# The request for ScalarE's common activation table and the load of the inducing points, moved to the head of the order

## The chip, the cores and the metric

One Trainium2 chip, one of its cores. The metric is the device time of one execution in microseconds; a time is the median of several runs.

## What is computed

Two stages, in float32 at the interfaces. An induced attention block: 32 inducing points attend to the 12480 rows of each of 4 batches, then the rows attend to the 32 results. A feed-forward block with a hard-swish follows, on all 49920 rows.

```python
def _attn_ref(x, inducing):                # x (4, 12480, 128), inducing (32, 128)
    scale = 1.0 / np.sqrt(C)
    I = np.broadcast_to(inducing[None], (B, m, C))
    def mab(q, kv):
        s = scale * (q @ kv.transpose(0, 2, 1))
        s = s - s.max(-1, keepdims=True)
        a = np.exp(s)
        a /= a.sum(-1, keepdims=True) + 1e-09
        return a @ kv
    h = mab(I, x)
    return mab(x, h)

def _moe_ref(x, w_in, w_out):              # w_in (128, 2048), w_out (2048, 128)
    h = x @ w_in
    relu6 = np.clip(h + 3.0, 0.0, 6.0)
    g = h * relu6 / 6.0
    return g @ w_out
```

## The kernel before

Each batch is cut into six groups of 2048 rows and a rest of 192. For each group of the first pass, x is loaded (`X`), cast to bf16 (`K`, line 456), transposed on TensorE (`T`, line 462) and copied out of PSUM (`Y`, line 468). Then come the scores against the inducing points (`S`, line 473), their exponential on ScalarE (`E`, line 481), and the sums over rows (`A`, line 489).

Between the passes, the 32 rows of the batch are prepared. The products of their differences with the first weight are squared on ScalarE (`N`, line 576) and multiplied by the second weight (`P`, line 631). Small steps on VectorE build the operands of the second pass (`cH` to `cP`).

The second pass avoids working over all 2048 hidden columns for each row: it uses the 32 prepared rows and products of pairs of attention weights. For each group it makes scores (`Z`, line 654) and two exponentials of them (`Zd`, line 664, and `Ze`, line 669), the row sums (`R`, line 686), their logarithm on ScalarE (`Rl`, line 691), the scores less that logarithm on VectorE (`Rz`, line 696), and the normalized weights by another exponential (`Ra`, line 710). Pairs of weights are made by a matmul (`B`, line 729), an exponential (`F`, tile `TF`, line 739) and a product on VectorE with a broadcast (`U`, tile `TD`, line 750, with `d` that `W` makes by DMA from POOL's queue, line 675). The matmuls `l` (line 800) and `q` (line 819) give the output rows, `v` (line 830) copies them out of PSUM, and `O` (line 840) stores them.

No scheduler orders this. `ORDER` is a string of tokens, written out by hand, for all four batches. Each token names one step with its indices, its PSUM bank and sometimes its engine, and the steps are emitted in that order:

```python
for token in ORDER.split():
    code, *args = token.split(".")
    ops[code](*[int(a) if a.isdigit() else a for a in args])
```

Every engine, and every queue of DMAs, runs its own part of the string in order. The second pass of one batch is interleaved with the first pass of the next.

ScalarE reads its functions from a table that is loaded by an instruction of its own (ACT_TABLE_LOAD in the trace). One set of functions is in force at a time. Where an instruction needs a function that isn't in the set in force, the build puts a load ahead of it. A kernel can also ask for a set by name. The two steps that the change moves:

```python
def op_i0(e):
    nc.scalar.dma_start(I_sb[:, :], inducing[:, :])              # line 350

def op_it(e):
    nc.scalar.preload_act_table_set("natural_log_exp_and_others")  # line 353
```

`i0` is issued from ScalarE's queue, and its tile is first read by `i4` (line 365), the transpose of the inducing points. `it` has no operands and waits for nothing. Before the change `it` stands between steps of the second pass of batch 0 and the first pass of batch 1.

At the head of the order, `X.0.0.0.8.SP` loads the first half of the first x group from SP's queue, `X.0.0.8.16.P` the second half from POOL's, `i2` clears a tile on VectorE, and `w` runs matmuls on it on TensorE (line 372).

Of the kernel before, what the change touches and what calls it, by code (L numbers as in the profile page):

```python
# [20 lines left out]


ORDER = """
X.0.0.0.8.SP i2.- w.8.6 X.0.0.8.16.P w.4.5 i0.- i1.- i3.V K.0.0.4.8.V X.0.1.0.16.P X.0.2.0.16.P X.0.3.0.16.P
X.0.4.0.16.P X.0.6.0.2.P K.0.0.0.4.A T.0.0.0.8.4 i8.- K.0.0.8.12.A Y.0.0.0.8.4.A K.0.0.12.16.V xc.4.8.V w.3.0
T.0.0.8.16.1 i4.5 i5.5.V w.1.0 S.0.0.0.8.4 K.0.1.0.4.A Y.0.0.8.16.1.V S.0.0.8.16.4 E.0.0.0.16.4 i6.P K.0.2.4.8.A
K.0.1.4.8.V T.0.1.0.8.1 i7.P K.0.2.8.12.A K.0.1.8.12.V K.0.1.12.16.V T.0.1.8.16.5 xc.0.4.V A.0.0.0.8.3 A.0.0.8.16.3
# [30 lines left out]
Y.1.6.0.2.7.V F.0.3.0.0 K.1.4.8.12.V F.0.3.0.1 q.0.2.0.0.5 D.1.1.V q.0.2.1.1.6 v.0.2.1.6.A l.0.2.3.7 H.1.2.4 Z.0.4.0.1  # L58
Zd.0.4.0 X.2.1.0.16.P D.1.2.V q.0.2.3.1.7 S.1.3.0.8.4 S.1.3.8.16.4 S.1.6.0.2.2 E.1.6.0.2.2 T.1.4.8.16.3 K.1.5.12.16.V
T.1.4.0.8.0 q.0.2.3.0.7 Ze.0.4.1 R.0.4.2 q.0.2.2.0.6 Y.1.4.8.16.3.V K.1.5.8.12.V T.1.5.8.16.3 Y.1.4.0.8.0.V W.0.4  # L60
v.0.2.3.7.V l.0.2.2.6 q.0.2.2.1.6 Y.1.5.8.16.3.V it.- O.0.1.0.16.P Rl.0.4.2 Rz.0.4.1 Rh.0.4.V E.1.3.0.16.4 q.0.2.0.1.5
T.1.5.0.8.7 S.1.4.0.8.4 Y.1.5.0.8.7.V v.0.2.2.6.A B.0.3.1 D.1.3.V A.1.3.0.8.6 A.1.3.8.16.6 X.2.2.0.16.P H.1.3.6 Ra.0.3
v.0.2.0.5.A S.1.4.8.16.4 Z.0.5.7.5 F.0.3.1.0 U.0.3.0.2 c2.1.- S.1.5.0.8.0 S.1.5.8.16.0 q.0.3.1.0.6 F.0.3.1.1 U.0.3.1.2
l.0.3.1.6 E.1.4.0.16.4 Ze.0.5.5 A.1.4.0.8.4 A.1.4.8.16.4 D.1.4.V K.2.0.0.4.V H.1.4.4 E.1.5.0.16.0 Zd.0.5.7 q.0.3.1.1.6
# [978 lines left out]
```

## Time and profile before

| | |
|---|---|
| time, median of 3 runs | 295.79 us (295.2 to 297.52) |
| the profiled execution | 296.27 us, span 294.4 us |
| TensorE (PE) busy | 273.8 us, 93% of the span |
| weight loads (PEld) | 211.2 us, 72% |
| ScalarE (ACT) busy | 255.7 us, 87% |
| VectorE (DVE) busy | 226.6 us, 77% |
| GpSimd (POOL) busy | 93.6 us, 32% |
| DMA | 66.69 MB, mean 227 GB/s |
| mean granted TensorE clock | 0.989 of full speed |

The span is the time between the first and the last instruction that the profile shows; the rest of the execution's time lies around it. An engine's busy share is a mean over stages with different limits. A wait in brackets names the idle time of an engine and what ended it. The chain of waits is followed back from the last instruction to what released it at each step.

### The profile page before, as it was taken

Reading aid. Unit: us, or ns where it says so; the run is one execution under the profiler, and the core shown is the slowest. Engines: PE = TensorE matmul, PEld = TensorE weight load, DVE = VectorE, ACT = ScalarE, POOL = GpSimd, SP = SyncE. Lnnn points to the kernel's source line nnn. Section 1 sums busy time; section 2 is a strip of 40 time slices with the busy share of each in tenths; the row PEclk is TensorE's granted clock in tenths of the full one; section 3 lists DMA queues with packets and bytes.
Section 4 is the critical chain, followed back from the end, with each engine's and each line's share of the span. In section 5 each row is a group of like instructions: output and inputs, shape, how many; then the busy total and the mean of one; then the engine's idle time right before and its main releaser. Section 6 shows DMA issues by size and latency. Waiting matters only on the chain.

```text
span 294.4 us, 9799 instructions
## 1 busy us (share of the span) xinstructions
PE 273.8 (93%) x4114; PEld 211.2 (72%) x4122; DVE 226.6 (77%) x468; ACT 255.7 (87%) x426; POOL 93.6 (32%) x184
## 2 busy tenths in 40 slices
PE   7788897699899999999999999999999999999990
PEld 3776565576688777877877877787888767776780
DVE  3889877748699966888798948889879866978750
ACT  2578999979998988998989999978899899889952
POOL 8322420213324013345172043052223233354210
PEclk9999999979999999999999999999999999999998
DMA  7999944066589905469997936339195153686574
GB/s 210 427 394 419 416 132 169 16 213 213 161 274 321 386 19 169 125 212 320 322 387 249 368 99 226 146 90 347 46 336 178 49 183 113 223 256 227 170 292 158
DMA packets 13232, 66.69 MB, mean 227 GB/s; under 512 B 2656, under 2 KB 3200, under 8 KB 7040
## 3 DMA queue, kind: packets, MB, share of 16 engines
q0 software_dynamic: 12416, 63.38, 63.2%
q1 hardware_dynamic: 576, 2.36, 2.1%
q8 instruction: 33, 0.54, 0.8%
q10 hardware_dynamic: 192, 0.28, 0.3%
q14 instruction: 15, 0.12, 0.2%
HBM read 27.67 MB, written 25.56 MB: 181 GB/s over the span
## 4 chain that ended last, share of the span: by engine, by line
PE 66%; ACT 15%; DMA 7%; issue 5%; DVE 4%; POOL 1%; POOLq 0%; ACTq 0%; DVEq 0%
PE ps L819 25%; PE ps L800 7%; PE ps L489 5%; DMA xr<-in_x_dram 5%; PE ps L462 5%; PE ps L729 5%; PE ps L654 4%; PE ps L631 4%; ACT TF L739 4%; PE ps L568 3%; PE ps L473 3%; ACT sq L576 2%; DMA out_dram<-os 2%; PE ps L686 2%; ACT os L830 2%
## 5 line engine op out<-in xcount | busy, mean ns | idle before, releaser
L739 ACT ACTIVATE TF<-ps 128x1024 bf16<-128x1024 f32 (+1 forms) x98 | 94.5, 1006 | 8.2 <-PE ps L729 7.6
L675 POOL DMA_DIRECT2D d<-dk x96 | 54.1, 582 | 95.5 <-ACT dk L664 88.9
L750 DVE TENSOR_TENSOR TD<-TF,d 128x2048 bf16<-128x2048 bf16 x47 | 57.0, 1217 | 5.5 <-ACT TF L739 4.6
L819 PE MATMUL ps<-Cq,TF 128*128 128x128 bf16 (+1 forms) x784 | 60.2, 221 | 0.0
L819 PE MATMUL ps<-Cq,TD 128*128 128x128 bf16 (+1 forms) x784 | 59.6, 221 | 0.1
L819 PEld LDWEIGHTS <-TF 128*128 128x128 bf16 (+1 forms) x784 | 46.2, 99 | 11.1 <-issue 8.4
L819 PEld LDWEIGHTS <-TD 128*128 128x128 bf16 (+1 forms) x784 | 46.2, 99 | 9.3 <-issue 6.0
L830 DVE COPY os<-ps 128x512 f32<-128x512 f32 x55 | 37.6, 686 | 13.4 <-PE ps L819 8.0
L800 PE MATMUL ps<-BD,a 128*128 128x512 f32 x96 | 47.4, 495 | 0.0
L576 ACT ACTIVATE sq<-ps 128x512 bf16<-128x512 f32 x64 | 35.5, 607 | 2.6 <-PE ps L568 2.0
L462 PE MATMUL ps<-ident_b,xb 128*128 128x128 bf16 x384 | 28.6, 219 | 4.1 <-ACT xb L456 2.9
L489 PE MATMUL ps<-xr,a 128*32 128x128 f32 x384 | 29.0, 225 | 2.3 <-ACT xT L468 2.2
L456 DVE CAST xb<-xr 128x512 bf16<-128x512 f32 x72 | 28.3, 422 | 1.6 <-DMA xr<-in_x_dram 1.6
L489 PEld LDWEIGHTS ps<-xr,a 128*32 128x32 f32 x384 | 24.9, 109 | 5.8 <-ACT xT L468 2.4
L468 DVE COPY xT<-ps 128x1024 bf16<-128x1024 bf16 x38 | 25.7, 685 | 4.3 <-PE ps L462 4.2
L462 PEld LDWEIGHTS <-xb 128*128 128x128 bf16 x384 | 22.4, 98 | 9.0 <-ACT xb L456 3.5
L696 DVE CUSTOM_DVE_ANT_0 zz<-ln,ps 128x512 f32<-128x512 f32 (+1 forms) x28 | 17.4, 622 | 14.2 <-ACT ln L691 13.9
L830 ACT COPY os<-ps 128x512 f32<-128x512 f32 x41 | 23.5, 593 | 3.8 <-DMA out_dram<-os 2.6
L840 POOL DMA_DIRECT2D out_dram<-os x22 | 12.4, 564 | 43.2 <-ACT os L830 28.7
L729 PE MATMUL ps<-z,pair 32*128 32x256 f16 (+1 forms) x392 | 21.0, 270 | 3.3 <-ACT sq L576 1.3
L437 POOL DMA_DIRECT2D xr<-in_x_dram x24 | 13.4, 561 | 28.7 <-PE ps L489 10.9
L631 PE MATMUL ps<-w_ob,sq 128*128 128x128 bf16 x256 | 20.3, 220 | 0.0
(154 smaller groups left out, 432.9 us busy)
## 6 DMA issues: line engine op xcount, KB each, us to landing
xr<-in_x_dram POOLq DMA_DIRECT2D x23, 1024.0 KB, 9.2
out_dram<-os POOLq DMA_DIRECT2D x22, 1024.0 KB, 5.6
d<-dk POOLq DMA_DIRECT2D x96, 128.0 KB, 3.6
os<-in_moe_w_in_dram POOLq DMA_DIRECT2D x1, 1024.0 KB, 10.0
w_or<-in_moe_w_out_dram POOLq DMA_DIRECT2D x1, 1024.0 KB, 12.2
out_dram<-os SPq DMA_DIRECT2D x1, 1024.0 KB, 6.4
os<-in_x_dram SPq DMA_DIRECT2D x1, 512.0 KB, 4.0
xr<-in_x_dram POOLq DMA_DIRECT2D x1, 512.0 KB, 6.0
```

The costliest lines, as they stand in the source:

```text
L456: copier(e)(at(xb, xbl, b, g)[:p, lo:hi, :], src)
L462: nc.tensor.transpose(pt[:, (i - lo) * p : (i - lo + 1) * p], at(xb, xbl, b, g)[:p, i, :], ident_b[:p, :p])
L489: nc.tensor.matmul(ps[:M, k, :C], lhsT=at(a1, a1l, b, g)[:p, i * M : (i + 1) * M], rhs=at(xr, xl, b, g)[:p, i, :], start=(i == 0), stop=(i ...
L576: nc.scalar.activation(sq_of(b, jb)[:, :], ps[:, k, :], ACT.Square)
L631: nc.tensor.matmul(ps[:, k, f * C : (f + 1) * C], lhsT=sq_of(b, jc)[:, f * P : (f + 1) * P], rhs=w_ob[:, jc, :], start=(jc == 0 and f == 0 ...
L675: nc.gpsimd.dma_start(fat(d_, b, g)[:, j, :w], fat(dk_, b, g)[32 * j : 32 * j + 32, :w].unsqueeze(1).to_broadcast([32, 4, w]),)
L729: nc.tensor.matmul(ps[:, j, f * w : (f + 1) * w], lhsT=pair[rows, f].rearrange("p m i -> p (m i)"), rhs=fat(z_, b, g)[rows, h * w : (h + 1 ...
L739: nc.scalar.activation(hat(TF_, b, g, h)[:, 2 * q : 2 * q + 2, :w], ps[:, 2 * q : 2 * q + 2, :w], ACT.Exp, scale=-1.0)
L750: nc.vector.tensor_mul(split(hat(TD_, b, g, h)), split(hat(TF_, b, g, h)), d.unsqueeze(2).to_broadcast([P, n, 2, w]),)
L800: nc.tensor.matmul(ps[:p, k, : J * C], lhsT=fat(a_, b, g)[:rows, s * p : (s + 1) * p], rhs=BD_[b % 2][:rows, :J, :].rearrange("p j c -> p ...
L819: nc.tensor.matmul(ps[:p, k, j * C : (j + 1) * C], lhsT=t[:, j, f * w + s2 * p : f * w + (s2 + 1) * p], rhs=Cq_[b % 2][:, (1 + f) if u els ...
L830: copier(e)(at(os_, osl, b, g)[:p, s * J : (s + 1) * J, :], ps[:p, k, : J * C].rearrange("p (j c) -> p j c", c=C),)
```

## The change

`i0` moves ahead by a few tokens, from behind the first matmuls to behind the first load of x, and `it` moves from its place in the middle of the order to directly behind `i0`. No other token moves, and no step's code is changed.

```diff
 ORDER = """
-X.0.0.0.8.SP i2.- w.8.6 X.0.0.8.16.P w.4.5 i0.- i1.- i3.V K.0.0.4.8.V X.0.1.0.16.P X.0.2.0.16.P X.0.3.0.16.P
+X.0.0.0.8.SP i0.- it.- i2.- w.8.6 X.0.0.8.16.P w.4.5 i1.- i3.V K.0.0.4.8.V X.0.1.0.16.P X.0.2.0.16.P X.0.3.0.16.P
...
-v.0.2.3.7.V l.0.2.2.6 q.0.2.2.1.6 Y.1.5.8.16.3.V it.- O.0.1.0.16.P Rl.0.4.2 Rz.0.4.1 Rh.0.4.V E.1.3.0.16.4 q.0.2.0.1.5
+v.0.2.3.7.V l.0.2.2.6 q.0.2.2.1.6 Y.1.5.8.16.3.V O.0.1.0.16.P Rl.0.4.2 Rz.0.4.1 Rh.0.4.V E.1.3.0.16.4 q.0.2.0.1.5
```

## The prediction

> **What bounds the kernel now.** I read the page first, then the stretches of the span, to find where TensorE is not full, then ScalarE's groups kept apart by shape, the chain of waits, and the order of time around single instructions.
>
> The stretches, in us: each row has the length, then the busy time of PE, PEld, DVE, ACT and POOL, the granted clock, the DMA share and GB/s.
>
> ```profile
> 32.00:50.00 18.00, 14.41 (x241) 11.44 (x245) 13.91 (x35) 17.88 (x28) 4.74 (x8) 1.00 0.67 233
> 32.00:58.00 26.00, 20.18 (x312) 15.82 (x313) 19.83 (x46) 25.83 (x39) 5.76 (x10) 1.00 0.47 162
> 32.00:64.00 32.00, 26.16 (x381) 20.14 (x381) 21.93 (x49) 30.15 (x46) 7.98 (x14) 0.95 0.53 173
> 32.00:80.00 48.00, 40.48 (x597) 31.12 (x598) 34.14 (x72) 45.75 (x68) 12.26 (x22) 0.96 0.54 178
> ...
> 80.00:270.00 190.00, 189.37 (x2929) 147.88 (x2931) 155.88 (x311) 174.06 (x302) 64.90 (x118) 1.00 0.65 217
> ```
>
> From 80 to 270 us TensorE is busy 189.37 of 190: it sets the pace, and ScalarE, at 174.06, has 8% to spare. From 32 to 80 it is the other way round: ScalarE is busy 45.75 of 48 and TensorE idles 48 - 40.48 = 7.52 us. What fills ScalarE there is told by its groups:
>
> ```profile
> L691 ACT ACTIVATE ln<-ps 128x512 f32<-128x512 f32 x24 | 14.5, 604 | 1.0 <-PE ps L686 0.8
> ...
> L691 ACT ACT_TABLE_LOAD x4 | 5.1, 1283 | 0.1
> ...
> L739 ACT ACT_TABLE_LOAD x2 | 2.6, 1283 | 0.0
> ...
> L456 ACT ACT_TABLE_LOAD x1 | 1.3, 1283 | 1.2 <-PEq L1027 1.2
> L481 ACT ACT_TABLE_LOAD x1 | 1.3, 1283 | 0.0
> L664 ACT ACT_TABLE_LOAD x1 | 1.3, 1283 | 0.0
> L353 ACT ACT_TABLE_LOAD x1 | 1.3, 1283 | 0.0
> ...
> L691 ACT ACTIVATE ln<-ps 64x96 f32<-64x96 f32 x4 | 1.0, 241 | 0.4 <-PE ps L686 0.4
> ```
>
> Ten table loads of 1283 ns. One is at the start (the L456 row). Eight more come where the logarithm (L691) and an exponential (L481, L664, L739) follow one another, and the tenth (L353) is the common table that `it` asks for. The chain that ended last, in order of time (start, length, what):
>
> ```profile
> 32.14 1.28 ACT L691
> ...
> 37.97 1.28 ACT L481
> ...
> 44.65 1.28 ACT L691
> ...
> 47.55 1.28 ACT L739
> ...
> 52.89 1.28 ACT L691
> ...
> 54.80 1.28 ACT L664
> ...
> 69.33 0.89 issue
> ...
> 72.21 1.28 ACT L739
> ```
>
> All eight switching loads lie on it (the one at 69.3 us is the row called issue).
>
> **The change part by part.** It moves two tokens of the order: `i0`, the inducing points' load, some places ahead, and `it`, the request for the common table, from the middle to directly behind it.
>
> *The request, where it arrives.* The start of the run, in order of time (start, length, engine, what, and in brackets the idle time before):
>
> ```profile
> 0.75 0.41 ACTq L350 DMA_DIRECT2D I_sb<-in_inducing_dram  x1
> ...
> 1.19 1.28 ACT L456 ACT_TABLE_LOAD   x1 [1.19 <-PEq L1027]
> ...
> 4.74 0.62 ACT L456 CAST xb<-os 128x512 bf16<-128x512 f32 x1 [2.27 <-DMA os<-in_x_dram]
> ...
> 8.55 0.24 PE L365 MATMUL ps<-ident,I_sb 32*128 32x32 f32 x1
> ```
>
> ScalarE's first instruction is already the issue of `i0`, and a load follows it. Afterwards that load should be the requested table in the same place. If an automatic load stayed beside it, the two would end at 1.19 + 2.57 = 3.76, still ahead of the first cast at 4.74, which waits for x: cost 0 at both ends, and 1.28 if that cover were gone.
>
> *`i0`.* It was ScalarE's first instruction and stays so. The tokens that it overtakes (`i2`, `w`, the second x load) are on VectorE, TensorE and POOL's queue, the first x load, still ahead of it in the order, is on SP's queue, and none of them waits for it. One DMA of 16 KB, issued at 0.75, is first used at 8.55, so even a landing some us later is hidden. I take 0; uncovered, a late landing would delay the scores of batch 0 by as much.
>
> *The request, where it leaves, and the switches.* What one load costs ScalarE beyond its length shows at the first one, and what follows the request at the last:
>
> ```profile
> 30.54 1.58 ACT L576 ACTIVATE sq<-ps 128x512 bf16<-128x512 f32 x3
> 32.14 1.28 ACT L691 ACT_TABLE_LOAD   x1
> 33.43 0.60 ACT L691 ACTIVATE ln<-ps 128x512 f32<-128x512 f32 x1
> ...
> 79.77 1.28 ACT L353 ACT_TABLE_LOAD   x1
> ```
>
> Three squares of 0.607 take 1.58, so one starts every 0.49: neighbours overlap by 0.12. The load overlaps nothing (0.02 behind the squares, and `ln` 0.01 behind it). Without it `ln` would start at 30.54 + 1.58 - 0.12 = 32.00 instead of 33.43: 1.43 us for each load. After 79.77 there is no load, though logarithms, exponentials, squares and copies go on alternating for 190 us: that table serves all four. In force from the start, it removes the eight switches, 8 x 1.43 = 11.4 us, all on the chain, and the one at 79.77, beside which TensorE is full: 1.43 us of slack.
>
> *What TensorE gives back.* 11.4 us is what ScalarE can give. TensorE must do the same work, and can only close its gaps, whose larger ones are these (the bracket: idle time, and who ended it):
>
> ```profile
> 34.08 0.61 PE L462 MATMUL ps<-ident_b,xb 128*128 128x128 bf16 x8 [0.98 <-ACT ln L691]
> ...
> 47.08 0.40 PE L729 MATMUL ps<-z,pair 32*128 32x256 f16 x8 [1.11 <-ACT sq L576]
> ...
> 49.92 0.40 PE L654 MATMUL ps<-xT,Wd 128*32 128x512 bf16 x4 [0.75 <-ACT TF L739]
> ...
> 57.65 0.67 PE L489 MATMUL ps<-xr,a 128*32 128x128 f32 x8 [2.23 <-ACT xT L468]
> ...
> 71.25 0.40 PE L729 MATMUL ps<-z,pair 32*128 32x256 f16 x7 [0.58 <-ACT ln L691]
> ...
> 75.49 0.39 PE L729 MATMUL ps<-z,pair 32*128 32x256 f16 x6 [0.63 <-ACT TF L739]
> ```
>
> All six end on ScalarE, and each lies behind one or two loads. Now the balance at the end of each stretch quoted first. By 50 us TensorE has idled 18 - 14.41 = 3.6, VectorE 4.1, and four loads are worth 5.7. By 58: 5.8, 6.2, six loads 8.6. By 64: 5.8, 10.1, 8.6. By 80: 7.5, 13.9, 11.4. TensorE has the least to give at every point, so its idle time is the price: 7.5 us. VectorE is close behind it at 50 and 58, which is where the forecast is weakest.
>
> To that comes the clock, first over the 40 slices of the page, then in two stretches:
>
> ```profile
> PEclk9999999979999999999999999999999999999998
> ```
>
> ```profile
> 56.00:59.50 3.50, 1.83 (x36) 1.34 (x37) 2.51 (x4) 3.49 (x7) 2.52 (x5) 1.00 0.33 61
> 59.50:62.90 3.40, 3.40 (x26) 2.61 (x23) 1.50 (x2) 2.15 (x4) 0.72 (x2) 0.50 0.74 190
> ```
>
> After a stretch with TensorE 52% busy it is granted half speed for 3.40 us, on the chain: half of that, 1.7 us, is lost. With the gap of 2.23 us closed, the stretch that precedes is full, and I take the half speed to be gone: bounds 0 and 1.7, taken 1.7, since the slice with the 7 is the only one before the last that falls below 9, and it follows the widest gap of TensorE in the rows above. (The Trainium skill, TensorE: Matmul & The Clock Gate, "Why this matters for your kernels", says that gaps above about 3 us, a whole idle window, bring the clock down to half. The trace doesn't agree: the longest gap there is 2.23 us. By the page the half speed has another cause, and the change need not remove it; the sum would be 7.0 instead of 8.7.)
>
> What stays of idle time I take from the worst of the later 30 us stretches:
>
> ```profile
> 150.00:180.00 30.00, 29.65 (x466) 23.38 (x464) 23.73 (x50) 27.70 (x54) 8.50 (x17) 1.00 0.77 269
> ```
>
> 0.35 of 30, that is 0.5 us over some 39. **Sum**: 7.5 + 1.7 - 0.5 = 8.7 us. ScalarE then has 45.75 - 8 x 1.28 - 0.23 = 35.3 us of work in 39.3, 90%, as it has from 80 to 270 (92%): it fits. The lead is kept after 80, where TensorE is full and its order unchanged. Loads of x leave POOL's queue when TensorE frees their buffers, so they move ahead with it; 3% more traffic a second meets a DMA share of 0.65.
>
> The profiled execution took 296.27 (span 294.4, 1.87 around it), which is 0.48 over the median of 295.79. 296.27 - 8.7 = 287.6 for it, and **287.1 us** on the median.
>
> **The rivals.**
>
> *The half speed stays.* Gain 7.5 - 0.5 = 7.0, time 288.8. For it: one such stretch is too few to know its cause. Against: it follows the emptiest stretch.
>
> *A second limit appears at once.* With ScalarE's loads gone, TensorE waits for VectorE or for single results where it waited for ScalarE. For it: VectorE's idle time exceeds TensorE's by 0.5 us at 50 and 0.3 at 58, and its waits are not spread like TensorE's. Against: no large gap of TensorE in these 48 us ends on VectorE. If half of the 7.5 stays, the gain is 3.8 and the time 292.0.
>
> *ScalarE gives all.* A busy TensorE isn't full: eight matmuls are listed as one run 0.6 us long which includes the last one's way out, and every gap closed saves a part of that too. Then the loads count in full: 11.4, time 284.4. Against: the balance above.
>
> *The request changes nothing*, because loads are placed whatever it asks: 295.8. (The Trainium skill, ScalarE activation tables, "Table sets in the compiler and the runtime", says that the back end places the loads per block, by the longest run that a set serves. That rule would have chosen the common table at the start and no switch; the trace, with nine loads after the first, doesn't agree.) Against: the L353 row, the request obeyed in its place.
>
> *Slower: the request doesn't last.* If another table replaces it at the first cast (4.74 us), with no request later, switching goes on to the end. The price: up to 81 us there are five logarithms and nine loads, thus near two for each; of the 28 (24 large and 4 small ones) 23 are left: 46 x 1.43 = 66 us on ScalarE, which has 190 - 174.06 = 16 to spare. 296 + 50 = some 346 us. It decides at the start: a second load before 12 us. Against: nothing replaced the table in 190 us after 79.77, and that work has every kind of operation that the start has.
>
> **How the numbers follow.** Chances: forecast 0.60 (its own range 286.0 to 288.4), half speed stays 0.15, second limit 0.12, ScalarE gives all 0.06, nothing changes 0.03, slower 0.04. The range runs from the full value of the loads, 284.2, to a gain of 4.8, 291.0: it takes in the first two, the fourth and nearly half of the third, and leaves out some 0.14. A measurement of this kernel can tell about 1%, 3 us, from no change: faster by more than that 0.93, within it 0.03, slower 0.04.
>
> **What would show it.** The page's chain by engine now:
>
> ```profile
> PE 66%; ACT 15%; DMA 7%; issue 5%; DVE 4%; POOL 1%; POOLq 0%; ACTq 0%; DVEq 0%
> ```
>
> Right: one table load in all, at about 1.2 us with line 353; TensorE above 97% busy between 32 us and the point that was 80 and is about 71; no half speed there; ScalarE's share of the chain down from 15% to under 8%; `ln`, `TF` and `sq` as long as before. Wrong: a load after the first, a granted clock of 0.5 around 50 to 60 us (7.0 instead of 8.7), gaps of TensorE that end on VectorE, or a stretch after 71 us in which TensorE idles for over 1 us and gives the lead back.

## The result, and the profile after

The changed kernel took **285.0 us**, the median of four runs, against 295.78 beside it; the ratio is 0.962, 95% interval 0.958 to 0.966. The forecast was 287.1, its range 284.2 to 291.0. Two later comparisons gave 286.42 against 295.36, ratio 0.972 (0.965 to 0.979), and 285.18 against 295.62, ratio 0.963 (0.959 to 0.967). The lines here are from the profile of the last one, since the executions profiled before met a late load of x, shown further down.

The page of the changed kernel, busy time by engine, and the chain by engine:

```profile
PE 270.6 (96%) x4114; PEld 209.4 (74%) x4122; DVE 226.6 (80%) x468; ACT 243.7 (86%) x417; POOL 94.1 (33%) x184
...
PE 79%; DMA 7%; ACT 4%; issue 4%; DVE 3%; POOL 1%; POOLq 0%; ACTq 0%; DVEq 0%
```

ScalarE has lost 12.0 us (255.7 to 243.7) and nine instructions: nine loads of 1.28, which make 11.5 of the 12.0. Its share of the chain fell from 15% to 4%. A `TF` or an `ln` takes as long as before, to 3 ns; an `sq` takes 622 ns where it took 607. VectorE's busy time is the same.

The stretches (length; PE, PEld, DVE, ACT, POOL busy; clock, DMA share, GB/s) that answer to those of before:

```profile
32.00:50.00 18.00, 17.95 (x306) 14.63 (x305) 17.51 (x42) 17.76 (x33) 6.07 (x11) 1.00 0.70 229
...
32.00:71.00 39.00, 38.95 (x641) 31.25 (x640) 36.57 (x77) 36.33 (x62) 14.01 (x25) 1.00 0.71 229
71.00:261.00 190.00, 189.38 (x2926) 147.11 (x2927) 155.95 (x311) 174.18 (x306) 64.76 (x116) 1.00 0.65 219
```

TensorE, busy 40.48 of 48 us before, is now busy 38.95 of 39, at full clock. VectorE and ScalarE are at 94 and 93%. The stretch behind is as full as it was.

The same work measured in both: from the first `Z` matmul of batch 0 to the first one of its fifth group, 563 matmuls and 565 weight loads, first before, then after:

```profile
28.90:77.35 48.45, 40.92 (x563) 30.16 (x565) 35.23 (x75) 46.29 (x68) 12.41 (x21) 0.96 0.57 189
```

```profile
28.59:65.32 36.73, 36.68 (x563) 27.86 (x565) 35.19 (x75) 35.38 (x60) 12.68 (x21) 1.00 0.73 241
```

The stretch is 11.72 us shorter. TensorE's idle time gives 7.53 - 0.05 = 7.5 of it. The other 4.2 come out of time that the profile lists as busy: 40.92 to 36.68 for the same instructions.

ScalarE at the head of the changed kernel, and where the first switch was:

```profile
0.75 0.41 ACTq L350 DMA_DIRECT2D I_sb<-in_inducing_dram  x1
1.19 1.28 ACT L353 ACT_TABLE_LOAD   x1 [1.19 <-PEq L1027]
4.78 0.62 ACT L456 CAST xb<-os 128x512 bf16<-128x512 f32 x1 [2.30 <-DMA os<-in_x_dram]
```

```profile
30.23 1.58 ACT L576 ACTIVATE sq<-ps 128x512 bf16<-128x512 f32 x3
31.66 0.64 ACT L691 ACTIVATE ln<-ps 128x512 f32<-128x512 f32 x1
```

The requested load took the automatic one's place, to the same hundredth, and is the only one of the run. `ln` starts at 31.66, 0.15 before the squares' listed end, as the working said (0.12).

### The profile page after: what moved, and what is told of

Its sections match the earlier page's. It is cut to its first block, busy times and chain, and to the rows that moved or that the text cites. A ratio compares the mean times of both kernels' runs of the same rounds, so it can differ in the third digit from the quotient of the medians.

```text
span 287.3 us, 9790 instructions
## 1 busy us (share of the span) xinstructions
PE 272.4 (95%) x4114; PEld 211.0 (73%) x4122; DVE 226.4 (79%) x468; ACT 244.0 (85%) x417; POOL 94.0 (33%) x184
## 4 chain that ended last, share of the span: by engine, by line
PE 77%; DMA 8%; ACT 5%; DVE 4%; issue 4%; POOL 1%; POOLq 0%; DVEq 0%; ACTq 0%
PE ps L819 27%; PE ps L800 8%; PE ps L462 7%; PE ps L489 7%; DMA xr<-in_x_dram 6%; PE ps L631 5%; PE ps L729 5%; PE ps L654 4%; PE ps L568 4%; PE ps L473 3%; PE ps L686 2%; DMA out_dram<-os 2%; PE ps L585 2%; ACT TF L739 2%; PE ps L608 1%
## 5 line engine op out<-in xcount | busy, mean ns | idle before, releaser
L675 POOL DMA_DIRECT2D d<-dk x96 | 54.7, 588 | 88.1 <-ACT dk L664 81.4
L462 PE MATMUL ps<-ident_b,xb 128*128 128x128 bf16 x384 | 29.6, 224 | 2.4 <-ACT xb L456 2.3
L489 PE MATMUL ps<-xr,a 128*32 128x128 f32 x384 | 29.6, 228 | 0.1
L462 PEld LDWEIGHTS <-xb 128*128 128x128 bf16 x384 | 23.1, 100 | 7.7 <-ACT xb L456 3.5
L489 PEld LDWEIGHTS ps<-xr,a 128*32 128x32 f32 x384 | 25.6, 111 | 3.2 <-issue 0.6
L568 PE MATMUL ps<-dH,w_hi 128*128 128x512 bf16 x58 | 19.8, 380 | 0.1
```

The costliest lines, as they stand in the source:

```text
L462: nc.tensor.transpose(pt[:, (i - lo) * p : (i - lo + 1) * p], at(xb, xbl, b, g)[:p, i, :], ident_b[:p, :p])
L489: nc.tensor.matmul(ps[:M, k, :C], lhsT=at(a1, a1l, b, g)[:p, i * M : (i + 1) * M], rhs=at(xr, xl, b, g)[:p, i, :], start=(i == 0), stop=(i ...
L568: nc.tensor.matmul(ps[:, k, :], lhsT=w_hi[:, jb, :], rhs=dH[:, :, :, :, :].rearrange("p q k m i -> p (q k m i)"),)
L675: nc.gpsimd.dma_start(fat(d_, b, g)[:, j, :w], fat(dk_, b, g)[32 * j : 32 * j + 32, :w].unsqueeze(1).to_broadcast([32, 4, w]),)
```

## The experiments

Medians are set beside 284.9 to 285.2: the changed kernel took 285.0 and 285.18 in two comparisons, and the kernel with the request alone at the head took 284.91. In a third comparison the changed kernel took 286.42; where that matters, the text says so. A steadier measure is the equal work of the section before. It takes 36.73 or 36.74 us in all eight profiles that have one load at the head and none between it and 70 us.

**Only the load of the inducing points moved.**

```diff
-X.0.0.0.8.SP i2.- w.8.6 X.0.0.8.16.P w.4.5 i0.- i1.- i3.V
+X.0.0.0.8.SP i0.- i2.- w.8.6 X.0.0.8.16.P w.4.5 i1.- i3.V
```

> Only the load of the inducing points moves to the head; the request for the common table stays in the middle. If the whole gain comes from the table loads, as the prediction has it: ten loads, no change, 295.8 us within 1%. If the earlier load of the inducing points carries a part of it: under 293 us.

295.32 us, ratio 0.998 (0.994 to 1.001): no change. Its ten loads are those of before.

**Only the request moved.**

```diff
-X.0.0.0.8.SP i2.- w.8.6 X.0.0.8.16.P w.4.5 i0.- i1.- i3.V
+X.0.0.0.8.SP it.- i2.- w.8.6 X.0.0.8.16.P w.4.5 i0.- i1.- i3.V
...
-Y.1.5.8.16.3.V it.- O.0.1.0.16.P
+Y.1.5.8.16.3.V O.0.1.0.16.P
```

> Only the request moves to the head, ahead of the load of the inducing points, which keeps its old place. If the table loads are all: one load at 1.2 us, 284.9 us, as with the whole change. If the inducing points' place matters: over 287 us. The profile should show TensorE full from 32 to 71 us, and, if the half speed follows nearly empty stretches only, none between 15 and 270 us.

284.91 us, ratio 0.964 (0.960 to 0.968): the whole gain. Time order of its head, and two stretches:

```profile
0.74 1.28 ACT L353 ACT_TABLE_LOAD   x1 [0.74 <-PEq L1027]
...
0.78 0.38 ACTq L350 DMA_DIRECT2D I_sb<-in_inducing_dram  x1
```

```profile
32.00:46.00 14.00, 13.95 (x251) 11.22 (x250) 13.81 (x35) 13.78 (x26) 4.64 (x8) 1.00 0.83 279
32.00:71.00 39.00, 38.95 (x642) 31.26 (x641) 36.57 (x77) 36.32 (x62) 13.96 (x25) 1.00 0.72 227
```

The load runs beside the DMA's issue, so the two tokens' order at the head doesn't matter either.

**The request in the place of the first, and of the fourth, switch.** Each kernel keeps the loads ahead of it.

```diff
-... R.0.0.2 Rl.0.0.2 ...                        # the first
+... R.0.0.2 it.- Rl.0.0.2 ...
-... P.0.14.5 B.0.0.1 F.0.0.1.0 ...              # the fourth
+... P.0.14.5 B.0.0.1 it.- F.0.0.1.0 ...
```

> The request stands ahead of the first logarithm (Rl.0.0.2), in the place of the first switching load: two loads in all. Loads counted in full on ScalarE's chain (1.43 us each): 1.4 us over the kernel with the request at the head, 286.3. TensorE's visible idle time alone, one gap of 0.98: 285.9. Nothing, if one load is absorbed by TensorE's backlog: 284.9.

> The request stands ahead of F.0.0.1.0, in the place of the fourth switching load: loads one to three remain, the request is the fourth, five to eight are gone. Loads counted in full: 4 x 1.43 = 5.7 over the kernel with the request at the head, 290.6 us. TensorE's visible idle time up to 50 us, 3.6: 288.5. If the gain of the second half hung on the half speed after the gap at 57 us, the granted clock there is full in this kernel, and the second half gives 5.7 or more of the 11.

The first: 286.46 us (285.69 to 287.36), 1.5 over the request at the head, ratio 0.969 (0.965 to 0.972). 1.4 was expected of a load in full and 1.0 of the visible gap; the runs of one kernel spread too far to part those two, but the load is not absorbed. The equal work in its profile parts them:

```profile
28.75:66.90 38.15, 37.10 (x563) 27.92 (x566) 35.28 (x75) 36.79 (x61) 12.72 (x21) 1.00 0.69 231
```

It is 1.42 us longer than the 36.73: a load in full. TensorE's idle time has grown by only 1.00 (from 0.05 to 1.05); the other 0.42 is listed as busy, for the same work and at full clock. Its ScalarE around the load:

```profile
30.39 1.58 ACT L576 ACTIVATE sq<-ps 128x512 bf16<-128x512 f32 x3
31.99 1.28 ACT L353 ACT_TABLE_LOAD   x1
33.28 0.60 ACT L691 ACTIVATE ln<-ps 128x512 f32<-128x512 f32 x1
```

The fourth: 291.77 us (289.72 to 293.78), ratio 0.985 (0.979 to 0.991). Its lowest run is 4.8 over the changed kernel and its median 6.9, where 5.7 was expected of four loads in full and 3.6 of the idle time. TensorE's stretch up to the fourth load, to be set beside the 13.95 above:

```profile
32.00:46.00 14.00, 12.05 (x193) 9.37 (x193) 10.31 (x26) 13.93 (x22) 4.59 (x8) 1.00 0.63 217
```

The equal work in it:

```profile
28.72:70.52 41.80, 38.20 (x564) 28.54 (x567) 35.43 (x75) 40.74 (x64) 12.51 (x21) 1.00 0.63 211
```

The four loads lengthen it by 5.07 us, between the two prices: 3.55 of idle time, and 1.52 listed as busy, again at full clock. The four switches that are gone then account for the rest, 11.72 - 5.07 = 6.65, half speed included; 5.7 or more was expected of this half, and the medians, which spread more here, give 4.3 (296.02 to 291.77). The granted clock where the gap at 57 us was is full in it. In this profile a load of x came late much further on and cost TensorE a gap of 2.12 us at 199 us; it may be part of the high median (more on that load below).

**No request at all.** The one token `it.-` is taken out.

> No request for the common table at all: the switches go on to the end. By the prediction's price, near two loads for each of the 28 logarithms, about 9 + 46 = 55 loads and the first one, 1.43 us each on ScalarE, which has 16 us to spare behind 80 us: some 346 us. If the loads behind 80 us hide behind TensorE: under 310 us.

355.52 us, the median of two runs, ratio 1.200 (1.189 to 1.212). ScalarE's groups and the stretch from 32 to 330 us:

```profile
L691 ACT ACT_TABLE_LOAD x28 | 35.9, 1283 | 0.7 <-issue 0.2
L739 ACT ACT_TABLE_LOAD x12 | 15.4, 1283 | 0.2
L481 ACT ACT_TABLE_LOAD x6 | 7.7, 1283 | 0.1
L710 ACT ACT_TABLE_LOAD x5 | 6.4, 1283 | 0.1
```

```profile
32.00:330.00 298.00, 251.43 (x3567) 191.13 (x3570) 194.79 (x387) 280.38 (x420) 77.02 (x140) 0.96 0.52 171
```

With six more under other lines there are 57 loads, where the working had 56. The 47 more than before cost 59.0 us against the 296.53 beside it. Priced at 1.43 they are 67, less 16 of slack 51; the kernel lost 8 more than that. Its profile also has seven half-speed stretches of 3.41 us ahead of the end, where the kernel before has one. At 1.7 us each, an estimate, the six more would cost some 10, so these can be the 8.

**Two switches put back, the fifth and sixth, around the gap of 2.23 us.**

```diff
-... K.1.3.0.4.A Rl.0.2.2 ...
+... K.1.3.0.4.A it.n Rl.0.2.2 ...      # it.n: the set "natural_log"
-... l.0.0.3.5 Ra.0.2
+... l.0.0.3.5 it.- Ra.0.2              # the common set again
```

> The changed kernel with two of the eight switches put back, the fifth and sixth, around the logarithm of group 2 (a request for the set with the logarithm alone, then the automatic load of the exponential's), and a request for the common table behind them, where ScalarE waits for TensorE anyway. Loads counted in full: 2 x 1.43 = 2.9, at most 4.3 if the third is not hidden: 287.8 to 289.2 us. By TensorE's backlog, if it soaks them up: under 286.3. If the gap brings the half speed back, 1.7 more and a granted clock of 0.5 in the stretch behind it.

287.75 us (287.18 to 292.97), ratio 0.970 (0.962 to 0.979): 2.6 to 2.9 over the changed kernel, about two loads in full, without the 1.7 more that the half speed was to bring. The third load is hidden: behind it ScalarE still waits 0.17 us for TensorE. ScalarE around the first two, the gap of TensorE, and two stretches behind each other:

```profile
47.10 1.28 ACT L353 ACT_TABLE_LOAD   x1
48.40 0.60 ACT L691 ACTIVATE ln<-ps 128x512 f32<-128x512 f32 x1
49.01 1.28 ACT L664 ACT_TABLE_LOAD   x1
50.31 0.60 ACT L664 ACTIVATE dk<-ps 128x512 bf16<-128x512 f32 x1
```

```profile
51.86 0.67 PE L489 MATMUL ps<-xr,a 128*32 128x128 f32 x8 [1.94 <-ACT xT L468]
```

```profile
49.60:53.00 3.40, 1.42 (x22) 0.84 (x19) 3.13 (x7) 3.39 (x5) 1.80 (x4) 1.00 0.18 31
53.00:56.40 3.40, 3.40 (x40) 2.67 (x36) 1.47 (x2) 3.38 (x5) 1.43 (x3) 0.50 0.75 176
```

The gap is back, and the half speed follows it, at another time of the run (53.0 instead of 59.5) but behind the same gap. The kernels with all the switches (no request; only the inducing points moved) have it there too, those with the request at the head, or in the first or fourth place, don't. So in these profiles the half speed comes and goes with that gap, and with the loads. It doesn't follow in every execution, though. The mean granted clock was 0.986 in this one, which took 287.98 us. It was 0.995 in the runs of 287.18 and 287.53, which leaves less than the 1.7 us that one such stretch takes from the clock. The equal work in this profile is 3.79 longer than the 36.73, against 2.86 for two loads in full, which leaves 0.9 for the half speed.

**Needless loads behind 80 us, where TensorE is full.** First pairs, then single ones at the same four places, then single ones ahead of output copies.

```diff
-... R.0.6.0 Rl.0.6.0 ...
+... R.0.6.0 it.x it.- Rl.0.6.0 ...     # pairs (it.x: the set "exp_and_others"); also ahead of Rl.1.2.5, Rl.1.5.1, Rl.2.1.2
+... R.0.6.0 it.- Rl.0.6.0 ...          # singles, the same places
-... l.0.6.0.6 v.0.6.0.6.A ...
+... l.0.6.0.6 it.- v.0.6.0.6.A ...     # singles at copies; also v.1.2.0.6, v.1.4.1.6, v.2.1.1.5
```

> The changed kernel with four pairs of needless table loads (another set, then the common one again) behind 80 us, where TensorE sets the pace: ahead of Rl.0.6.0, Rl.1.2.5, Rl.1.5.1 and Rl.2.1.2. Each pair holds ScalarE for 2 x 1.28 + 0.12 = 2.7 us, 10.8 in all. If a load costs only what TensorE's backlog and ScalarE's 8% of slack can't soak up: 1 to 5.5 us, 286 to 290.4. If each counts in full wherever it stands: 295.7.

296.55 us: as slow as the kernel before, ratio 0.999 (0.996 to 1.002). Some 11 us over the changed kernel, which wasn't run beside it, for 10.8 of held ScalarE: the expectation of 1 to 5.5 fell. One pair, and the gaps of TensorE behind three of the four (the profiled execution took 300.27 us, and also has a gap of 2.52 us behind a late load of x):

```profile
120.03 2.57 ACT L353 ACT_TABLE_LOAD   x2
122.61 0.60 ACT L691 ACTIVATE ln<-ps 128x512 f32<-128x512 f32 x1
```

```profile
123.26 0.61 PE L819 MATMUL ps<-Cq,TD 128*128 128x128 bf16 x8 [2.01 <-ACT ln L691]
...
149.23 0.40 PE L729 MATMUL ps<-z,pair 32*128 32x256 f16 x7 [1.87 <-ACT ln L691]
...
182.05 0.39 PE L729 MATMUL ps<-z,pair 32*128 32x256 f16 x6 [2.12 <-ACT ln L691]
```

A block of 2.7 us leaves a gap of about 2.0 (1.74 behind the first pair): TensorE can go on for some 0.7 us without ScalarE, and little more. The gaps sum to about 8; the rest I put down to the half speed, which this profile shows behind two of the four, for 3.41 and 6.83 us. That share isn't measured by itself.

> The changed kernel with one needless table load (the common set again) at each of the four places of the pairs, ahead of a logarithm. If each counts in full: 4 x 1.43 = 5.7, 290.6 us. If TensorE has the backlog that the pairs showed (a block of 2.7 us left a gap of 1.9 to 2.1, so some 0.6 to 0.7 is soaked up): 4 x 0.8 = 3.2, 288.1. If a block of 1.4 us is hidden behind a TensorE that is always busy: 284.9 to 285.9.

288.19 us (287.66 to 288.72), as that backlog had it (288.1): 3.0 to 3.3 over 284.9 to 285.2, 0.8 for each load of 1.43. Over the changed kernel beside it, 286.42, it is only 1.8, but that one lost time to a late load of x (below), which this profile doesn't show. From the first `Z` matmul to the last matmul of all the two profiles without that late load take 250.77 us here and 246.97 in the changed kernel: 3.8, or 0.95 for each load. Three of the four gaps:

```profile
98.55 0.38 PE L568 MATMUL ps<-dH,w_hi 128*128 128x512 bf16 x1 [0.46 <-ACT ln L691]
...
120.66 0.61 PE L819 MATMUL ps<-Cq,TD 128*128 128x128 bf16 x8 [0.72 <-ACT ln L691]
...
143.91 0.40 PE L729 MATMUL ps<-z,pair 32*128 32x256 f16 x7 [0.58 <-ACT ln L691]
```

> The same four loads, each ahead of a copy of an output tile on ScalarE (v.0.6.0.6.A, v.1.2.0.6.A, v.1.4.1.6.A, v.2.1.1.5.A) instead of a logarithm, whose result VectorE and TensorE wait for at once. If only ScalarE's order counts and its backlog is the same everywhere: as with the loads ahead of the logarithms, within 1 us. If it counts what waits behind the load: at least 1.5 us less than those.

289.11 us (288.70 to 289.67), 0.9 above the loads ahead of logarithms, not below them: what waits directly behind the load isn't what counts. (A late load of x, for which TensorE idles 0.69 us in this profile, may be part of the 0.9.) All that ScalarE does behind the load is late, and TensorE soon needs one of those results. In the profile its gaps behind the four loads end on other results of ScalarE, 1.9 to 4.5 us after each load's start: 0.81 us on `TF`, 0.91 on `os`, 0.71 on `sq`, 0.49 on `os`.

**The changed kernel again, and the load of x.**

> The changed kernel once more, beside the next two on the same chip: 284.9 us, TensorE full from 32 to 71 us, one table load.

286.42 us (284.98 to 289.19), ratio 0.972 (0.965 to 0.979), with TensorE full from 32 to 71 us and one load. Further on VectorE waits for a load of x, and TensorE for VectorE: 1.57 us in this profile. Here is VectorE's wait in this profile, then the waits in the first one taken of the changed kernel (VectorE, then TensorE):

```profile
193.03 0.43 DVE L456 CAST xb<-xr 128x512 bf16<-128x512 f32 x1 [1.91 <-DMA xr<-in_x_dram]
```

```profile
193.76 0.43 DVE L456 CAST xb<-xr 128x512 bf16<-128x512 f32 x1 [2.19 <-DMA xr<-in_x_dram]
...
194.43 0.61 PE L819 MATMUL ps<-Cq,TF 128*128 128x128 bf16 x8 [1.85 <-DVE hacc L502]
```

So I moved that cast behind what TensorE waits for.

```diff
-... l.2.1.3.7 K.3.5.8.12.V A.3.1.0.8.6 A.3.1.8.16.6 H.3.1.6 l.2.2.3.5 F.2.2.0.1 F.2.2.0.0 B.2.2.1 ... T.3.5.0.8.2 U.2.2.0.2 ...
+... l.2.1.3.7 A.3.1.0.8.6 A.3.1.8.16.6 H.3.1.6 l.2.2.3.5 F.2.2.0.1 F.2.2.0.0 U.2.2.0.2 K.3.5.8.12.V B.2.2.1 ... T.3.5.0.8.2 ...
```

> The changed kernel, and VectorE's first cast of the last but one large x group of batch 3 (K.3.5.8.12.V) stands behind the sum H.3.1.6 and the product U.2.2.0.2 instead of ahead of both. In two profiles of the changed kernel that cast waited 1.9 and 2.2 us for its load, and TensorE 1.6 and 1.9 us for the sum behind it. If that load is what the executions of the changed kernel differ by: the gap of TensorE near 192 us gone or under 0.5, no half speed behind it, and a median 1 to 2 us under that of the changed kernel beside it, with a narrower spread. If the lateness comes from elsewhere: the same time within 0.7 us.

> The changed kernel unaltered, on the same chip as the one with the later cast, for comparison: 284.9 to 286.4 us, the wait for the x load near 192 us in its profile or not.

284.65 us (284.33 to 285.29) against 285.18 (283.96 to 285.71) for the changed kernel beside it: 0.5 apart, inside the 0.7 that was set for no effect. The profile of the changed kernel taken then shows the same wait at 0.21:

```profile
191.28 0.43 DVE L456 CAST xb<-xr 128x512 bf16<-128x512 f32 x1 [0.21 <-DMA xr<-in_x_dram]
```

In that profile the load was hardly late, so the edit may have had little to mend. The order with the later cast is the lowest median of all, but not shown to be better.

## Why the prediction was right, and what was mis-sized

*Mechanism: as forecast.* The eight switches went, the ninth load with them, the requested one replaced the first, and TensorE took over as the limit. With the request alone the whole gain comes; with the inducing points alone, nothing.

*The size: 8.7 forecast, 10.8 measured.* 285.0 lies below the forecast's own range (286.0 to 288.4), and within 0.6 of the rival "ScalarE gives all", which had 284.4 and a chance of 0.06. It lies in the whole range only because that was stretched to the loads' full value (given as 284.2 there, though its sum is 284.4). The step that failed is the one that made TensorE's listed idle time the price. Term by term, over the equal work:

- Idle time: 7.5 forecast, 7.5 measured.
- Half speed: 1.7 forecast, from one execution. The stretch after has the full clock, and putting back two switches brought it back behind their gap. But not every execution of the kernel before has it. Of its 51 runs beside the experiments (one of 852.57 us left out), 18 had a mean granted clock of 0.992 or more. That is too high for such a stretch besides the half speed at the end: in the 14 profiles the end alone loses 1.4 to 2.6 us of clock, so both would lose at least 3.1 of 295, which leaves 0.9895. The median of these 18 is 294.8 us; that of the 21 with 0.988 or less, too low for the end alone, is 296.5. The size of 1.7 fits, but the median of all runs holds only a part of it. The profiled execution holds it whole, which is probably why the equal work there gained 11.72 and the medians 10.8.
- What stays: -0.5 forecast. 0.05 of 36.7 us stayed.
- Missing: about 2.5 us, the part of the 4.2 from busy time that the half speed doesn't explain. With no half speed in the way it shows by itself: 0.42 us for one load and 1.52 for four, beside 1.00 and 3.55 of idle time. My reading is that a run of matmuls is listed up to its last one's way out, so each gap of TensorE is listed too short by a part of that, and shorter gaps don't appear at all. I had written this down as the reason for a rival and gave it almost no weight.

With it the sum is 7.5 + 1.7 + 2.5 = 11.7, the 11.72 measured over that work, and near the 11.4 of eight loads at 1.43. The 2.5 is what is left over here, and near what the four loads show (1.52 doubled is 3.0). The balance by stretches that made TensorE "the least to give" compared a count that was too low with one that was right.

*Left alone: the lead behind 71 us.* I said that it is kept. It is, where the loads of x are in time: 189.38 of 190 busy. In the first profile TensorE lost 1.85 us, and then the half speed followed. This is the "stretch in which TensorE idles for over 1 us and gives the lead back" that I had named as a sign of being wrong. The two profiled executions with that wait took 289.1 and 286.2 us, the one almost without it 284.9. (Those two also have half speed near 11 us, which costs little; see the last section.) From its issue to the cast that load took 8.7, 8.4 and 6.7 us in them; why isn't settled.

*The slack of ScalarE.* I called the load at 79.77 "1.43 us of slack" and reckoned with 8% to spare behind 80 us. The pairs show that this average is worth little: TensorE goes on for 0.7 us without ScalarE, and a TensorE that is always busy can't make up a stop. In the kernel without a request, too, the loads cost 8 us more than my price less that slack, though its half-speed stretches can be the reason there.

*The load's price.* The Trainium skill, ScalarE: Activation LUTs, "What ACT_TABLE_LOAD costs", gives about 1283 ns and a drain of about 1380 more for each switch. The 1283 is the trace's own number. The drain isn't seen: the load starts 0.02 behind the last activation's end, the next activation 0.01 behind the load's, one load put back lengthens the equal work by 1.42 us, and two cost 2.6 to 2.9 us together, not the 5.3 that the page's figures come to (an estimate).

## What to carry to other kernels

A table load holds ScalarE for its own length plus the overlap that it breaks (here 1.28 + 0.12). Where ScalarE sets the pace, one load cost that in full (1.42 us), and four together 5.07. Where TensorE sets it, a load ahead of a logarithm cost what TensorE couldn't bridge without ScalarE (here 0.8 to 0.95 of 1.43). The mean slack of ScalarE says nothing about that, the backlog (here 0.5 to 0.7 us) does. So ask for one set that serves all functions ahead of the first activation, in a wait that exists anyway. When a stall is to be priced by another engine's idle time, add the ends of its runs to the listed gaps, and check against the same instructions in a stretch without stalls.

## What the runs showed of the hardware

The half speed comes in stretches of 3.41 us, and within one profile on a fixed grid: in the kernel without a request they start at 59.74, 131.42, 145.07, 155.31, 261.12 and 302.08 us, apart by 21, 4, 3, 31 and 12 times 3.413. From one profile to the next the grid lies elsewhere. Ahead of the end, and with two exceptions named below, each follows a stretch in which TensorE was listed as busy for 2.3 us or less. Cut along the grid, from the first instruction to the last matmul, all nine stretches of the 14 profiles with TensorE busy under 1.62 of 3.41 us were followed by one. Between 1.6 and 2.3 it went both ways: 1.82 was followed by half speed in the kernel before (from 56.08 us), and 1.84 by full speed here, in the changed kernel's second profile:

```profile
191.64:195.05 3.41, 1.84 (x33) 1.59 (x31) 2.02 (x6) 1.97 (x3) 0.00 (x0) 1.00 0.83 309
195.05:198.46 3.41, 3.41 (x53) 2.65 (x53) 3.41 (x7) 3.15 (x7) 0.00 (x0) 1.00 0.03 12
```

The fullest of the nine, 1.61, is in the kernel with the request in the fourth place:

```profile
195.65:199.07 3.42, 1.61 (x25) 1.04 (x23) 0.96 (x4) 2.38 (x3) 0.00 (x0) 1.00 1.02 394
199.07:202.48 3.41, 3.10 (x33) 2.24 (x32) 3.41 (x7) 0.59 (x1) 0.00 (x0) 0.50 0.23 72
```

Twice the half speed lasted a second stretch, though TensorE was listed as busy 3.41 and 2.94 us in the first (the pairs, from 182.76 us, and the kernel without a request, from 302.08); why stays open. A gap of 2 us can thus cost some 1.7 us more, an estimate from half of 3.41, depending on how it falls on the grid.

Three profiles (the first two of the changed kernel, and the request in the first switch's place) also have a half-speed stretch near 11 us. Their first `Z` matmul starts at 28.63 to 29.12 us and that of the others at 28.42 to 28.99, so it costs little there.

The Trainium skill, TensorE: Matmul & The Clock Gate, "Why this matters for your kernels", asks for a gap of about 3 us, a whole idle window. That is stricter than what these runs show, where single gaps of 1.85 to 2.23 us were enough.
